# Down projection of the second token half by Strassen's seven products with a running sum each

## The chip, the cores and the metric

The kernel runs on one core of a Trainium2 chip. The metric is the device time of one execution in microseconds (us); lower is better.

## The reference

An adaLN block: attention with a layer norm and modulation from a condition vector, then a gated MLP with the same. Only the MLP's last step is touched.

```python
h = _layernorm(x, axis=-1) * (1 + cb) + sb            # x: 2048 tokens x 576
gate = jnp.einsum("bsd,df->bsf", h, W_gate)           # 576 x 4608
up = jnp.einsum("bsd,df->bsf", h, W_up)
gate = gate * (gate > 0)
x = x + gb * jnp.einsum("bsf,fd->bsd", gate * up, W_down)   # 4608 x 576
```

## The kernel before, in words

All matmuls run in a 4-byte format that keeps fewer bits than float32, so each operand is cut into `hi` (a cast, on ACT) and `lo` (the rest, a subtraction on POOL), and a product is three matmuls: hi by hi, hi by lo, lo by hi.

The MLP goes over the tokens in two halves of 1024, and in each half over the 4608 hidden columns in 18 blocks of 256: 36 blocks `m`, of which 18 to 35 (`m >= NFP`) are the second token half. A block has two column tiles `f` and two token quarters `k` of 512. Gate and up of a block are computed by Strassen's scheme (in Winograd's form) in seven products P1, P6, P2, P7, P5, P4, P3, in this order. Each product has a gate half (`xx` = 0) and an up half (`xx` = 1), written by `prod` into the two banks of one PSUM pair (tile `gu`); each half is 7 matmuls of 128x512. P2 adds onto P1's banks and P3 onto P5's.

`evac` empties a pair after both halves: P1 by an ACT copy into `q`, P6 and P7 by one DVE addition of 1024 columns, P2 by two DVE operations, P5, P4 and P3 by three of 512 columns each. P2, P5, P4 and P3 give the hidden tiles `r`, which `h_out` cuts into `hhi` and `hlo`.

The down projection of block `m` runs one block later, between the half-products of `m + 1`: 8 pieces `md_piece`, one for each 128 tokens, each of 12 matmuls 128x288 (two column halves, two `f`, three terms) into the pair `w` of pool `psW`, which has one buffer. DVE then adds the piece to `acc` (16 tiles of 128 x 576, residual and result). The down weights `wogb` are cut once in the first token half, stored in DRAM (`dk`) and loaded again in the second (`wd_prep`).

PE, DVE, ACT and POOL keep the order in which the code issues; semaphores come from the tiles that instructions share. `mat(m, s, fn)` places extra work in slot `s + 1` of block `m`, after the first half-product of that slot; `mlp_slots` writes the order out. SP issues the loads.

Of the kernel before, what the change touches and what calls it, by code (L numbers as in the profile page):

```python
# [21 lines left out]
NFT = F // P  # L22
# [3 lines left out]
H2 = D // 2  # L26
# [5 lines left out]
def kernel(  # L32
# [13 lines left out]
    nc = tc.nc  # L46
# [18 lines left out]
    dr = ctx.enter_context(tc.tile_pool(name="dr", bufs=1, space=bass.MemoryType.DRAM))  # L65
# [32 lines left out]
    acc = []  # L98
# [137 lines left out]
    mods = {}  # L236
# [185 lines left out]
    qhi, qlo, pthi, ptlo, ohi, olo = {}, {}, {}, {}, {}, {}  # L422
# [25 lines left out]
    st_, t4, t5, pt, hi_, lo_, bc, rb, rinv, ks_, pvps, done, o, bps = ({} for _ in range(14))  # L448
# [192 lines left out]
    NFP = NFT // 2  # L641
    NB = 2 * NFP
    ds_, hhi, hlo = {}, {}, {}
    wop, wraw, hop = {}, {}, {}
    pair, tmp = {}, {}

    def md_piece(m, k, qt, pool=None):
        b, fp = divmod(m, NFP)
        i = 8 * b + 4 * k + qt
        down_piece([hhi[m, f, k] for f in range(2)], [hlo[m, f, k] for f in range(2)],  # L650
                   [ds_[m, f] for f in range(2)], i, qt, f"md{m}_{k}_{qt}", pool=pool)()
        if fp == NFP - 1:
            nc.sync.dma_start(out[i * P:(i + 1) * P, :], acc[i])


    OPS = {"P1": ("A11", "B11"), "P2": ("A12", "B21"), "P6": ("S2", "T2"), "P7": ("S3", "T3"),
           "P5": ("S1", "T1"), "P4": ("A22", "T4"), "P3": ("S4", "B22")}
# [6 lines left out]
    dkeep = [dr.tile([P, 2, D], F32R, name=f"dk{f}") for f in range(NFT)]  # L664
    stores = []

    def flush_stores(left=0, eng=None):
# [258 lines left out]
    def prod(m, s, n, xx):  # L926

        hs, w = hop[m // NFP, OPS[s][1]], wop[n]
        ps = pair[m, s][:, xx, :]
# [10 lines left out]
    def h_out(m, f, k, r):  # L940
        pool, tag = HI[f, k]
        hi = hhi[m, f, k] = pool.tile([P, 512], F32R, tag=tag, name=f"hhi{m}_{f}{k}")
        if k == 0:
            pool, tag, w = op, "olo", 512
        elif f == 1:
            pool, tag, w = qp, ("qlo", "qhi")[m % 2], 512
        else:
            pool, tag, w = xp, "xm", 640
        lo = hlo[m, f, k] = pool.tile([P, w], F32R, tag=tag, name=f"hlo{m}_{f}{k}")[:, :512]
        nc.scalar.copy(hi, r)  # L950
        nc.gpsimd.tensor_sub(lo, r, hi.bitcast(F32))  # L951

    def gated(m, f, k, ps, r, a, op1=ALU.add):

        if a is None:
            nc.vector.tensor_scalar(r, ps[:, 0, :], 0.0, None, op0=ALU.max)
        else:
            nc.vector.tensor_tensor(r, ps[:, 0, :], a[:, 0, :], op=ALU.add)
            nc.vector.tensor_tensor(ps[:, 1, :], ps[:, 1, :], a[:, 1, :], op=op1)
        nc.vector.scalar_tensor_tensor(r, r, 0.0, ps[:, 1, :], op0=ALU.max, op1=ALU.mult)  # L960
        h_out(m, f, k, r)


    npair, px, free, kind = [0], {}, ["s", "s"], {}

# [5 lines left out]
    def new_pair(m, s):  # L971
        pair[m, s], kind[m, s] = new_banks(f"gu{npair[0]}")

    def evac(m, s):
        ps = pair[m, s]
        if s == "P1":
            t = tmp["q"] = pp.tile([P, 2, 512], F32, tag="hi", name=f"q{m}")
            nc.scalar.copy(t, ps)
        elif s == "P2":
            gated(m, 0, 0, ps, xp.tile([P, 640], F32, tag="xm", name=f"r{m}")[:, :512], None)  # L980
        elif s == "P6":
            nc.vector.tensor_tensor(tmp["q"], ps, tmp["q"], op=ALU.add)
        elif s == "P7":
            t = tmp["r"] = pp.tile([P, 2, 512], F32, tag="lo", name=f"r{m}", bufs=2)
            nc.vector.tensor_tensor(t, ps, tmp["q"], op=ALU.add)
            nc.scalar.copy(tmp["q"][:, 1, :], ps[:, 1, :])
        elif s == "P5":
            t = pp.tile([P, 2, 512], F32, tag="lo", name=f"c22_{m}", bufs=2)
            gated(m, 1, 1, ps, t[:, 0, :], tmp["r"])
        elif s == "P4":  # L990
            gated(m, 1, 0, ps, tmp["r"][:, 0, :], tmp["r"])
        else:

            gated(m, 0, 1, ps, tmp["q"][:, 0, :], tmp["q"], ALU.subtract)

    def wd_prep(m, f):
        tag = "wB" if f else "wC"
        k = 2 * (m % NFP) + f
        if m < NFP:
            load, gate, cut = prep_out(ds_, k, wd, "gb", (m, f), (None, tag))  # L1000

            def keep():
                cut()
                stores.append((dkeep[k], ds_[m, f][2]))

            return load, gate, keep

        def back():
            w = wp.tile([P, 2, D], F32R, tag=tag, name=f"wogb_{m}_{f}")
            ds_[m, f] = (w[:, 0, :], w[:, 1, :])  # L1010
            nc.sync.dma_start(w.bitcast(F32), dkeep[k].bitcast(F32))

        return [back]

# [171 lines left out]
    for i, ab in enumerate(lay0 + lay):  # L1186
        n = i - len(lay0) - 2 * NFT + 4
# [7 lines left out]
    for m in range(NB):  # L1195
        for f in range(2):
            for k, fn in enumerate(wd_prep(m, f)):
                if m >= NFP:
                    at_ = m, 3 * f
# [4 lines left out]
                mat(*at_, fn, sums=k == 1)  # L1204
    for i in range(4):
# [262 lines left out]
```

## Time and profile before

| what | value |
|---|---|
| runs | 2969.05, 2975.15, 2975.42 us; median 2975.15 us |
| span of the profiled execution | 2973.3 us (the page gives no other time for it) |
| PE busy over the span | 2895.3 us, 97% |
| DVE, ACT, POOL busy | 71%, 46%, 63% |
| second half's steady blocks (2500 to 2930 us) | PE 430.0 of 430 us, DVE 194.0, ACT 50.6, POOL 63.4 |

A timeline row has start, duration, engine, line, operation, output <- inputs and count; in brackets stand the idle time before it and the releaser. Matmuls are pipelined, so a row's duration reaches past the start of the next one; what PE needs is read from start to start.

### The profile page before, as it was taken

How to read it: one execution, taken by the hardware profiler on the slowest of the kernel's cores; microseconds unless marked ns; L12 is line 12 of the kernel's file. 1: busy time of each engine (PE TensorE's matmuls, PEld its weight loads, DVE VectorE, ACT ScalarE, POOL GpSimd, SP SyncE). 2: the span in 40 equal slices, each digit the busy share in tenths (PEclk: the TensorE clock that was granted, in tenths of full speed). 3: DMA queues.
4: the chain of work that ended last, by engine and by line, in shares of the span. 5: the costliest groups of instructions: out<-in, count | busy, mean ns of one | idle time of the engine just before them, and what ended most of it. 6: DMA issues, size and time to landing. Idle time of an engine off the chain costs nothing.

```text
span 2973.3 us, 41247 instructions
## 1 busy us (share of the span) xinstructions
PE 2895.3 (97%) x15448; PEld 2524.8 (85%) x15448; DVE 2108.3 (71%) x2894; ACT 1369.6 (46%) x1877; POOL 1866.1 (63%) x1309
## 2 busy tenths in 40 slices
PE   6889999999999999999999999999999999999999
PEld 5678888888888888888888788888878888888888
DVE  5778888788778888777889577777786444444444
ACT  3656666666676666666656333333323111111110
POOL 3767888888888889866777666678777211111111
PEclk8999999999999999999999999999999999999999
DMA  5312222222223223222243466668768844445443
GB/s 181 117 68 87 86 86 83 67 102 90 91 84 105 89 67 131 99 73 78 74 140 134 144 231 241 244 259 286 262 240 286 308 165 165 161 170 175 160 165 111
DMA packets 170759, 438.90 MB, mean 148 GB/s; under 512 B 15808, under 2 KB 62656, under 8 KB 170560
## 3 DMA queue, kind: packets, MB, share of 16 engines
q1 hardware_dynamic: 133200, 298.66, 30.3%
q10 hardware_dynamic: 37360, 137.61, 11.6%
q8 instruction: 122, 2.00, 0.3%
q14 instruction: 77, 0.63, 0.1%
HBM read 285.25 MB, written 179.27 MB: 156 GB/s over the span
## 4 chain that ended last, share of the span: by engine, by line
PE 86%; DVE 6%; POOL 3%; DMA 2%; ACT 2%; issue 2%; SPq 0%; ACTq 0%; DVEq 0%; POOLq 0%
PE gu L935 24%; PE md L590 15%; PE wo L590 13%; PE qps L387 12%; PE s L463 3%; PE s L462 3%; PE s L461 3%; PE pv L565 3%; PE pv L564 3%; PE pv L563 3%; DVE wr L741 2%; POOL lo L545 1%; PE qm L489 1%; DMA hop_T<-hk_T 1%; DVE t L466 1%
## 5 line engine op out<-in xcount | busy, mean ns | idle before, releaser
L545 POOL TENSOR_TENSOR lo<-p,hi 128x1024 fp32r<-128x1024 f32 x256 | 611.4, 2410 | 0.0
L554 POOL TENSOR_TENSOR ks<-ks,p 128x512 f32<-128x512 f32 x256 | 343.5, 1342 | 284.9 <-ACT p L538 211.4
L601 DVE TENSOR_TENSOR acc<-md,acc 128x576 f32<-128x576 f32 x288 | 217.7, 756 | 391.1 <-PE md L590 390.1
L590 PE MATMUL md<-wogb,hhi 128*128 128x288 f32 x2304 | 471.1, 297 | 14.3 <-DVE acc L601 14.3
L590 PEld LDWEIGHTS md<-wogb,hhi 128*128 128x128 f32 x2304 | 386.2, 189 | 39.6 <-DVE acc L601 18.5
L466 DVE TRANSPOSE_TENSOR_REDUCE t<-s 128x32 f32<-128x1024 f32 x256 | 316.2, 1243 | 136.0 <-PE s L463 125.0
L935 PE MATMUL gu<-hop_B,wop 128*128 128x512 f32 (+1 forms) x1512 | 373.1, 394 | 0.2
L590 PE MATMUL md<-wogb,hlo 128*128 128x288 f32 x1152 | 341.2, 296 | 0.0
L951 POOL TENSOR_TENSOR hlo<-r,hhi 128x512 fp32r<-128x512 f32 x72 | 93.7, 1301 | 372.4 <-issue 240.8
L935 PEld LDWEIGHTS gu<-hop_B,wop 128*128 128x128 f32 (+1 forms) x1512 | 279.8, 189 | 55.2 <-ACT lflh L920 0.9
L935 PE MATMUL gu<-hop_T,wop 128*128 128x512 f32 (+1 forms) x1260 | 314.3, 394 | 0.6 <-DMA wop<-wk_P 0.6
L536 DVE TENSOR_TENSOR p<-s,mb 128x1024 f32<-128x1024 f32 x250 | 295.3, 1219 | 4.2
L387 PE MATMUL qps<-hTa,wA 128*128 128x512 f32 x1176 | 285.7, 394 | 4.8 <-ACT wA L185 2.5
L590 PE MATMUL wo<-woga,ohi 128*128 128x288 f32 x1344 | 280.1, 302 | 0.0
L525 ACT CAST hi<-p 128x1024 fp32r<-128x1024 f32 x256 | 269.0, 1051 | 7.0
L538 ACT ACTIVATE p<-p 128x1024 f32<-128x1024 f32 x250 | 264.0, 1056 | 17.6 <-DVE p L536 15.7
L935 PEld LDWEIGHTS gu<-hop_T,wop 128*128 128x128 f32 (+1 forms) x1260 | 232.3, 189 | 44.2 <-DMA wop<-wk_P 1.0
L387 PEld LDWEIGHTS qps<-hTa,wA 128*128 128x128 f32 x1176 | 223.4, 190 | 53.4 <-ACT wA L185 2.9
L950 ACT CAST hhi<-r 128x512 fp32r<-128x512 f32 x72 | 44.7, 621 | 447.2 <-DVE r L960 443.8
L441 ACT ACTIVATE qhi<-qps 128x512 fp32r<-128x512 f32 x128 | 76.5, 597 | 341.8 <-PE qps L387 341.8
L590 PEld LDWEIGHTS wo<-woga,ohi 128*128 128x128 f32 x1344 | 218.8, 189 | 6.6
L590 PEld LDWEIGHTS md<-wogb,hlo 128*128 128x128 f32 x1152 | 217.4, 189 | 0.0
(207 smaller groups left out, 6408.4 us busy)
## 6 DMA issues: line engine op xcount, KB each, us to landing
wop<-wk_P SPq DMA_DIRECT2D x133, 640.0 KB
wk_P<-wop ACTq DMA_DIRECT2D x119, 640.0 KB
wr<-wlay SPq DMA_DIRECT2D x68, 384.0 KB
dk<-wogb ACTq DMA_DIRECT2D x36, 576.0 KB
wogb<-dk SPq DMA_DIRECT2D x36, 576.0 KB
againq<-akq SPq DMA_DIRECT2D x22, 640.0 KB
againo<-ako SPq DMA_DIRECT2D x18, 576.0 KB
rogb<-wd SPq DMA_DIRECT2D x36, 288.0 KB
```

The costliest lines, as they stand in the source:

```text
L387: return [lambda i=i, a=a, b=b: nc.tensor.matmul(ps, a, b, start=(i == 0), stop=(i == n - 1)) for i, (a, b) in enumerate(ops)]
L461: nc.tensor.matmul(ps, k[:, kt, :], qhi[u], start=True, stop=False)
L466: nc.vector.tensor_reduce(t4[u][:, 2 * h:2 * h + 2, :].rearrange("p k b -> p (k b)"), t.rearrange("p k (b j) -> p (k b) j", j=32), axis=AX ...
L525: nc.scalar.copy(hi_[u, h], pt[u, h])
L536: nc.vector.tensor_tensor(p, t, bc[u][:, None, :].to_broadcast([P, 2, 512]), op=ALU.subtract)
L538: nc.scalar.activation(p, p, AF.Exp, bias=0.0, scale=1.0)
L545: nc.gpsimd.tensor_sub(lo_[u, h], pt[u, h], hi_[u, h].bitcast(F32))
L554: nc.gpsimd.tensor_tensor(ks_[u], ks_[u], p[:, j, :], op=ALU.add)
L590: nc.tensor.matmul(ps[:, half, :H2], a[:, sl], w[b][:, cs], start=(n == 0 and seed is None), stop=(n == 5), skip_group_check=seed is not None)
L601: nc.vector.tensor_tensor(av, ps[:, :, :H2], av, op=ALU.add)
L935: nc.tensor.matmul(ps, a, c, start=s not in ("P2", "P3") and i == 0, stop=i == len(ops) - 1, skip_group_check=True)
L951: nc.gpsimd.tensor_sub(lo, r, hi.bitcast(F32))
```

## The change

For blocks 18 to 33 (`FAST`) the down projection is Strassen's too. The hidden block is 2 x 2 of (column tile, token quarter), the down weights 2 x 2 of (row tile, column half of 288). Seven products of 512 tokens by 288 columns take the place of eight: 84 matmuls 128x288 in a block instead of 96.

- **Pieces.** `fast_piece` makes 14 pieces of 6 matmuls, two column halves each: kind "4" (A22, two token groups), "16" (A11 and S2), "75" (S3 and S1), "23" (A12 and S4). One is issued after each half-product.
- **Running sums.** Each product is summed over the 16 blocks in a tile of its own: `acc` 0 to 7, free by then, take "16" and "75"; "4" and "23" go straight to `acc` 8 to 15. In the first such block ACT copies "16" and "75" into `acc`, later DVE adds. After block 33 `fast_end` mixes the sums on POOL and adds them on DVE, in slots of blocks 34 and 35.
- **Hidden tiles.** Four sums on POOL (S1, S2, S3, S4) and seven splits (`fast_split`) a block instead of four.
- **Weights.** The raw `wd` tile is loaded again, gated, combined and cut on POOL and ACT (`fast_weights`); `dk` keeps only the 4 tiles of blocks 34 and 35.
- **Evacuation.** In all blocks from 18, `evac_half` takes the place of `evac`: each half is emptied on its own, the first between the two half-products.

```diff
+    def fast_piece(m, kind, n):
+        if kind == "4":
+            specs = [(fop[m, "A22"], fw[m, "4"], 0, 2 * n + j) for j in range(2)]
+        else:
+            a, b = {"16": ("A11", "S2"), "75": ("S3", "S1"), "23": ("A12", "S4")}[kind]
+            specs = [(fop[m, x], fw[m, kind], j * H2, n) for j, x in enumerate((a, b))]
+        ps = psW.tile([P, 2, 512], F32, tag="w", name=f"mf{m}_{kind}_{n}")
+        for j, ((hi, lo), (whi, wlo), c, qt) in enumerate(specs):
+            sl = slice(qt * P, (qt + 1) * P)
+            for i, (x, w) in enumerate(((hi, whi), (hi, wlo), (lo, whi))):
+                nc.tensor.matmul(ps[:, j, :H2], x[:, sl], w[:, c:c + H2], start=i == 0, stop=i == 2)
...
+        if kind != "23" and m == FAST[0]:
+            nc.scalar.copy(a, ps[:, :, :H2])
+        else:
+            nc.vector.tensor_tensor(a, ps[:, :, :H2], a, op=ALU.add)
...
+    def fast_split(m, name, raw):
...
+        nc.scalar.copy(hi, raw)
+        nc.gpsimd.tensor_sub(lo, raw, hi.bitcast(F32))
...
+    def fast_weights(m):
...
+        mat(m - 1, 6, load)
+        mat(m, 0, lambda: gate(1))
+        mat(m, 1, lambda: gate(0))
+        mat(m, 1, sums1)
+        mat(m, 2, sums2)
+        mat(m, 2, cut4)
+        mat(m, 3, lambda: cut("16"))
+        mat(m + 1, 0, lambda: cut("75"))
+        mat(m + 1, 1, lambda: cut("23"))
+
+    def fast_end():
...
+        def put(n):
+            for a, b in ((acc[12 + n], acc[n]), (acc[8 + n], acc[4 + n])):
+                nc.vector.tensor_tensor(a, a, b, op=ALU.add)
...
+    def gated_half(x, ps, r, a, op1=ALU.add):
+        if x == 0:
+            if a is None:
+                nc.vector.tensor_scalar(r, ps[:, 0, :], 0.0, None, op0=ALU.max)
+            else:
+                nc.vector.tensor_tensor(r, ps[:, 0, :], a[:, 0, :], op=ALU.add)
+            return
+        if a is not None:
+            nc.vector.tensor_tensor(ps[:, 1, :], ps[:, 1, :], a[:, 1, :], op=op1)
+        nc.vector.scalar_tensor_tensor(r, r, 0.0, ps[:, 1, :], op0=ALU.max, op1=ALU.mult)
+
+    def fast_later(m):
...
+        nc.gpsimd.tensor_add(s1, r21, tmp[m, "r22"])
+        nc.gpsimd.tensor_sub(s2, s1, r11)
+        nc.gpsimd.tensor_sub(r11, r11, r21)
+        fast_split(m, "S2", s2)
+        fast_split(m, "S1", s1)
+        fast_split(m, "S3", r11)
...
+    def evac_half(m, s, x):
+        ps, fast = pair[m, s], m in FAST
+        if s == "P1":
+            if x == 0:
+                tmp[m, "q"] = pp.tile([P, 2, 512], F32, tag="hi", name=f"q{m}")
+            else:
+                nc.scalar.copy(tmp[m, "q"], ps)
+                if m - 1 in FAST:
+                    fast_last(m - 1)
+            return
+        q = tmp[m, "q"]
+        if s == "P6":
+            nc.vector.tensor_tensor(q[:, x, :], ps[:, x, :], q[:, x, :], op=ALU.add)
+            return
...
+            if m - 1 in FAST:
+                md = fast_pieces(m - 1)
...
                     others(m, i)
-                if m and i:
+                if m >= NFP:
+                    evac_half(m, s, 0)
+                if m and i or m - 1 in FAST:
                     md.pop(0)()
...
                 prod(m, s, 7 * m + i, 1)
                 wop.pop(7 * m + i)
-                if m and i < 2:
+                if m >= NFP:
+                    evac_half(m, s, 1)
+                if m and i < 2 or m - 1 in FAST:
                     md.pop(0)()
...
-                evac(m, s)
+                if m < NFP:
+                    evac(m, s)
```

How it moves instructions. First PE in a block of the second half, at product P5: the end of its first half, a down piece, the start of its second half. `gu` is the pair, `hop` the tokens' operand, `wop` the gate and up weights. In brackets stand the semaphores that an instruction waits for. Before:

```order
L935 MATMUL gu_24498<-hop_T_4_22907,wop_24434 128x512
L935 MATMUL gu_24498<-hop_T_2_22905,wop_24434 128x512
L590 MATMUL md_1_1_24510<-wogb_0_24121,hhi_01_24342 128x288 [waits DVE_49]
L590 MATMUL md_1_1_24510<-wogb_0_24121,hhi_01_24342 128x288
L590 MATMUL md_1_1_24510<-wogb_0_24121,hlo_01_24343 128x288
L590 MATMUL md_1_1_24510<-wogb_1_24240,hhi_11_24267 128x288 x2
L590 MATMUL md_1_1_24510<-wogb_1_24240,hlo_11_24268 128x288
L590 MATMUL md_1_1_24510<-wogb_0_24121,hhi_01_24342 128x288 x2
L590 MATMUL md_1_1_24510<-wogb_0_24121,hlo_01_24343 128x288
L590 MATMUL md_1_1_24510<-wogb_1_24240,hhi_11_24267 128x288 x2
L590 MATMUL md_1_1_24510<-wogb_1_24240,hlo_11_24268 128x288
L935 MATMUL gu_24498<-hop_T_0_22903,wop_24434 128x512 x2
```

Now, the same place (`mf_75` is a piece of kind "75", `fw` its weights, `fp_S` the split sums):

```order
L1043 MATMUL gu_24622<-hop_T_2_22840,wop_24539 128x512
L669 MATMUL mf_75_2_24637<-fw_75_24503,fp_S_24399 128x288 [waits DVE_49]
L669 MATMUL mf_75_2_24637<-fw_75_24503,fp_S_24399 128x288 x2
L669 MATMUL mf_75_2_24637<-fw_75_24503,fp_S_24396 128x288 x3
L1043 MATMUL gu_24622<-hop_T_0_22839,wop_24539 128x512 [waits DVE_49]
L1043 MATMUL gu_24622<-hop_T_0_22839,wop_24539 128x512
L1043 MATMUL gu_24622<-hop_T_3_22842,wop_24539 128x512
L1043 MATMUL gu_24622<-hop_T_1_22840,wop_24539 128x512 x2
```

The piece has six matmuls instead of twelve, and the second half's first matmul now waits for a DVE semaphore, the one that the evacuation of the first half of the same pair raises.

DVE in block 24, from a down piece's add before P2 to the evacuation of P5 (`r` and `c22` are hidden tiles). Before:

```order
L601 TENSOR_TENSOR acc11_136<-md23_0_3_24704,acc11_136 128x576
L956 TENSOR_SCALAR r24_24725<-gu128_24614 128x512
L960 SCALAR_TENSOR_TENSOR r24_24725<-r24_24725,gu128_24614 128x512
L601 TENSOR_TENSOR acc12_137<-md23_1_0_24742,acc12_137 128x576
L985 TENSOR_TENSOR r24_24763<-gu130_24732,q24_24645 128x1024
L601 TENSOR_TENSOR acc13_138<-md23_1_1_24778,acc13_138 128x576
L958 TENSOR_TENSOR c22_24_24799<-gu131_24766,r24_24763 128x512
L959 TENSOR_TENSOR gu131_24766<-gu131_24766,r24_24763 128x512
L960 SCALAR_TENSOR_TENSOR c22_24_24799<-c22_24_24799,gu131_24766 128x512
```

Now, the same stretch of block 25:

```order
L1074 TENSOR_SCALAR r25_25156<-gu133_25053 128x512
L679 TENSOR_TENSOR acc2_127<-mf24_16_2_25158,acc2_127 128x576
L1080 SCALAR_TENSOR_TENSOR r25_25156<-r25_25156,gu133_25053 128x512
L679 TENSOR_TENSOR acc3_128<-mf24_16_3_25178,acc3_128 128x576
L1115 TENSOR_TENSOR r25_25203<-gu135_25186,q25_25065 128x512
L679 TENSOR_TENSOR acc4_129<-mf24_75_0_25205,acc4_129 128x576
L1115 TENSOR_TENSOR r25_25203<-gu135_25186,q25_25065 128x512
L679 TENSOR_TENSOR acc5_130<-mf24_75_1_25222,acc5_130 128x576
L1076 TENSOR_TENSOR c22_25_25243<-gu136_25230,r25_25203 128x512
L679 TENSOR_TENSOR acc6_131<-mf24_75_2_25245,acc6_131 128x576
L1079 TENSOR_TENSOR gu136_25230<-gu136_25230,r25_25203 128x512
L1080 SCALAR_TENSOR_TENSOR c22_25_25243<-c22_25_25243,gu136_25230 128x512
```

An add now stands after each half's evacuation, and P7's one operation of 1024 columns has become two of 512.

ACT in block 19, where block 18's first pieces are emptied (`fh` are casts of hidden tiles, `fw` of weights):

```order
L1104 COPY q19_23241<-gu103_23229 128x1024
L695 CAST fh18_A12_23259<-q18_22946 128x512
L695 CAST fh18_S4_23264<-q18_22946 128x512
L734 CAST fw18_75_23287<-ft18_23030 128x576
L677 COPY acc0_125<-mf18_16_0_23292 128x576
L677 COPY acc1_126<-mf18_16_1_23308 128x576
L734 CAST fw18_23_23325<-fr18_22934 128x576
L677 COPY acc2_127<-mf18_16_2_23334 128x576
L695 CAST fh19_A22_23350<-r19_23332 128x512
L677 COPY acc3_128<-mf18_16_3_23354 128x576
```

The copies that free the pair `w` stand behind casts, of which S4's reads a sum that POOL makes; before, no such copy was on ACT.

More of the change, by code (lines that the diff above doesn't have):

```diff
@@ new lines, in fast_end, with mix @@
+    def fast_end():
+        def mix(n):
+            e1, e2 = acc[n], acc[4 + n]
+            nc.gpsimd.tensor_add(e1[:, H2:], e1[:, H2:], e1[:, :H2])
+            nc.gpsimd.tensor_add(e2[:, :H2], e2[:, :H2], e1[:, H2:])
+            nc.gpsimd.tensor_add(e1[:, H2:], e1[:, H2:], e2[:, H2:])
+            nc.gpsimd.tensor_add(e2[:, H2:], e2[:, H2:], e2[:, :H2])
+        def put(n):
+            for a, b in ((acc[12 + n], acc[n]), (acc[8 + n], acc[4 + n])):
+                nc.vector.tensor_tensor(a, a, b, op=ALU.add)
+        last = FAST[-1] + 1
+        for n in range(4):
+            mat(*((last, 5), (last, 6), (last + 1, 0), (last + 1, 1))[n], lambda n=n: mix(n))
+            mat(last + 1, 2 + n, lambda n=n: put(n))
@@ L663 @@
     wkeep = {(fp, s): dr.tile([P, 2, 5, P], F32R, name=f"wk{fp}_{s}") for fp in range(NFP) for s in OPS}
-    dkeep = [dr.tile([P, 2, D], F32R, name=f"dk{f}") for f in range(NFT)]
+    dkeep = [dr.tile([P, 2, D], F32R, name=f"dk{f}") for f in range(NFT - 2 * len(FAST))]
     stores = []
@@ new lines, in fast_later, with fast_last @@
+    def fast_later(m):
+        r21, s1 = tmp[m, "r"][:, 0, :], tmp[m, "r"][:, 1, :]
+        r11, s2 = tmp[m, "c"][:, 0, :], tmp[m, "c"][:, 1, :]
+        nc.gpsimd.tensor_add(s1, r21, tmp[m, "r22"])
[4 more added lines that the diff above has]
+        fast_split(m, "S3", r11)
+    def fast_last(m):
+        r12, s4 = tmp[m, "q"][:, 0, :], tmp[m, "q"][:, 1, :]
+        fast_split(m, "A12", r12)
+        nc.gpsimd.tensor_sub(s4, r12, tmp[m, "c"][:, 1, :])
+        fast_split(m, "S4", s4)
@@ new lines, in evac_half @@
+    def evac_half(m, s, x):
[3 more added lines that the diff above has]
+                tmp[m, "q"] = pp.tile([P, 2, 512], F32, tag="hi", name=f"q{m}")
+            else:
+                nc.scalar.copy(tmp[m, "q"], ps)
[5 more added lines that the diff above has]
+            nc.vector.tensor_tensor(q[:, x, :], ps[:, x, :], q[:, x, :], op=ALU.add)
+            return
+        if s == "P7":
+            if x == 0:
+                tmp[m, "r"] = pp.tile([P, 2, 512], F32, tag="lo", name=f"r{m}", bufs=2)
+            nc.vector.tensor_tensor(tmp[m, "r"][:, x, :], ps[:, x, :], q[:, x, :], op=ALU.add)
+            if x:
+                nc.scalar.copy(q[:, 1, :], ps[:, 1, :])
+            return
+        if s == "P2" and x == 0:
+            tmp[m, "r22"] = xp.tile([P, 640], F32, tag="xm", name=f"r{m}")[:, :512]
+        if s == "P5" and x == 0:
+            tmp[m, "c"] = pp.tile([P, 2, 512], F32, tag="lo", name=f"c22_{m}", bufs=2)
+        f, k, r, a, op1 = {"P2": lambda: (0, 0, tmp[m, "r22"], None, ALU.add),
+                           "P5": lambda: (1, 1, tmp[m, "c"][:, 0, :], tmp[m, "r"], ALU.add),
+                           "P4": lambda: (1, 0, tmp[m, "r"][:, 0, :], tmp[m, "r"], ALU.add),
+                           "P3": lambda: (0, 1, q[:, 0, :], q, ALU.subtract)}[s]()
+        gated_half(x, ps, r, a, op1)
+        if x == 0:
+            return
+        if not fast:
+            h_out(m, f, k, r)
+        elif s == "P2":
+            fast_split(m, "A22", r)
+        elif s == "P5":
+            fast_split(m, "A11", r)
+        elif s == "P4":
+            fast_later(m)
@@ L1003, in keep @@
                 cut()
-                stores.append((dkeep[k], ds_[m, f][2]))
+                if m + NFP not in FAST:
+                    stores.append((dkeep[k - 2 * len(FAST)], ds_[m, f][2]))
             return load, gate, keep
@@ L1195 @@
     for m in range(NB):
+        if m in FAST:
+            fast_weights(m)
+            continue
         for f in range(2):
```

53 lines of the change are left out of this document (51 added, 2 removed).

## The prediction

> **What bounds the kernel now.** I read the page's totals first, then the busy time by stage, then the chain of waits and the order of time in the stage that the change touches. In the stages, the columns are span, then busy time of PE, PEld, DVE, ACT, POOL, then PEclk, DMA share and GB/s.
>
> ```profile
> PE 2895.3 (97%) x15448; PEld 2524.8 (85%) x15448; DVE 2108.3 (71%) x2894; ACT 1369.6 (46%) x1877; POOL 1866.1 (63%) x1309
> 1750.00:2050.00 300.00, 296.28 (x1633) 260.15 (x1632) 212.05 (x240) 110.19 (x160) 207.32 (x191) 1.00 0.69 254
> 2160.00:2230.00 70.00, 63.09 (x333) 55.35 (x332) 57.85 (x47) 19.77 (x27) 54.72 (x47) 0.95 0.64 234
> 2500.00:2930.00 430.00, 430.00 (x2368) 381.11 (x2367) 193.96 (x255) 50.58 (x74) 63.38 (x49) 1.00 0.48 164
> ```
>
> The last row is the second token half of the MLP. PE has no gap in 430 us; DVE is at 45%, ACT at 12%, POOL at 15%. There each PE instruction removed is time saved, and each wait added to PE is time lost. The chain repeats the same piece once in each block m:
>
> ```profile
> 2531.78 4.83 PE gu L935 x21
> ...
> 2919.85 4.83 PE gu L935 x21
> ```
>
> Eleven blocks lie between, so a block is 388.07 / 11 = 35.28 us. What it is made of:
>
> ```profile
> 2642.28 0.43 PE L590 MATMUL md<-wogb,hhi 128*128 128x288 f32 x2
> 2642.48 1.01 ACT L978 COPY q<-gu 128x1024 f32<-128x1024 f32 x1 [0.28 <-PE gu L935]
> ...
> 2643.88 1.77 PE L935 MATMUL gu<-hop_T,wop 128*128 128x512 f32 x7
> 2644.08 0.76 DVE L601 TENSOR_TENSOR acc<-md,acc 128x576 f32<-128x576 f32 x1 [2.61 <-PE md L590]
> 2645.48 0.43 PE L590 MATMUL md<-wogb,hhi 128*128 128x288 f32 x2
> ```
>
> A down piece of 12 matmuls takes 2643.88 - 2642.28 = 1.60 us from start to start, a half-product of 7 takes 1.60 (1.605 in longer runs): 8 x 1.60 + 14 x 1.605 = 35.27, the block.
>
> **What is removed.** In 16 blocks 8 pieces of 12 matmuls become 14 of 6. By the rows above a piece of 6 is 0.80, and 14 x 0.80 = 11.2 instead of 12.8: 1.60 us a block, **25.6 us** in all. A block's two wogb loads become one raw load, and 32 dk stores go. No wait on these loads shows in the stage, so I count the DMA at nothing; 0.48 of DMA share is the cover, and it only falls.
>
> **What is added to POOL, ACT and DVE.** The prices:
>
> ```profile
> L951 POOL TENSOR_TENSOR hlo<-r,hhi 128x512 fp32r<-128x512 f32 x24 | 31.1, 1295 | 209.6 <-issue 167.4 <-ACT hhi L950 42.2
> L186 POOL TENSOR_TENSOR wogb<-rogb,wogb 128x576 fp32r<-128x576 f32 x17 | 24.1, 1420 | 0.0
> L950 ACT CAST hhi<-r 128x512 fp32r<-128x512 f32 x24 | 14.9, 621 | 209.9 <-DVE r L960 209.9
> L959 DVE TENSOR_TENSOR gu<-gu,r 128x512 f32<-128x512 f32 x17 | 11.9, 700 | 0.9
> L959 DVE TENSOR_TENSOR gu<-gu,r 128x512 f32<-128x512 f32 x24 | 16.8, 699 | 0.8
> ```
>
> POOL, a block: 7 splits and 4 sums of 512 (11 x 1.295), 2 gates and 3 cuts of 576 (5 x 1.42), 5 operations of 288 (estimated at half of 1.42 each): 14.2 + 7.1 + 3.6 = 24.9 us of 35. ACT: seven casts of 0.62 and the weights' casts, some 8 us. DVE: 12 adds of 0.76, four of 288 columns, 15 operations of about 0.69: 21 us. None is full. The last two rows are the same DVE operation beside a POOL at 69% (207.32 of 300) and at 15% (63.38 of 430): 700 and 699 ns, so more POOL work does not slow an operation that reads one bank and one SBUF tile, which all the steady ones are. POOL's queue has slack too. Its result that is wanted soonest after it is made is the cut of weights "75". P1's second half ends 9.9 us after P4's (four half-products, four pieces and P3's wait, below); then come the q copy and a cast on ACT (1.0 + 0.6), three POOL operations of 1.295 with a cast of 0.6 between, and the cut of 1.42: 17.5. The first piece that reads it stands three products on, at some 22.5. I count POOL and ACT at nothing in steady blocks; were those 5 us used up, PE would wait at that piece.
>
> **The new wait.** The order shows what the diff does not: the second half of each product waits for DVE's evacuation of the first half, though that lies in the other bank of the tile. Only a 6-matmul piece (0.80) stands between. The rows for the price of that round trip:
>
> ```profile
> 2663.11 3.38 PE L935 MATMUL gu<-hop_T,wop 128*128 128x512 f32 x14
> 2664.97 0.69 DVE L958 TENSOR_TENSOR c<-gu,r 128x512 f32<-128x512 f32 x1 [0.90 <-PE gu L935]
> ...
> 2669.52 1.78 PE L935 MATMUL gu<-hop_B,wop 128*128 128x512 f32 x7
> 2669.72 0.69 DVE L958 TENSOR_TENSOR r<-gu,r 128x512 f32<-128x512 f32 x1 [0.85 <-PE gu L935]
> 2670.45 0.70 DVE L959 TENSOR_TENSOR gu<-gu,r 128x512 f32<-128x512 f32 x1
> 2671.14 0.43 PE L590 MATMUL md<-wogb,hhi 128*128 128x288 f32 x2
> 2671.18 0.69 DVE L960 SCALAR_TENSOR_TENSOR r<-r,gu 128x512 f32<-128x512 f32 x1
> ```
>
> DVE starts 0.20 after PE goes on (2669.72 - 2669.52), or 0.26 where it waits for a second engine too (half of the fourteen ends at 2664.71; the operation starts at 2664.97). The operation takes 0.69 to 0.70. The way back:
>
> ```profile
> 2258.47 0.74 DVE L601 TENSOR_TENSOR acc<-md,acc 128x576 f32<-128x576 f32 x1
> 2259.26 0.54 PE L590 MATMUL md<-wogb,hhi 128*128 128x288 f32 x2 [0.62 <-DVE acc L601]
> ...
> 2260.97 1.78 PE L935 MATMUL gu<-hop_B,wop 128*128 128x512 f32 x7
> ```
>
> PE goes on 0.05 after DVE ends (2259.21 to 2259.26), and the piece then takes 1.71 instead of 1.60, since the weight load in front of a held matmul is no longer covered: 0.11 more. The same is seen at a product:
>
> ```profile
> 1916.37 1.28 POOL L713 TENSOR_TENSOR wop<-ws,wop 128x512 fp32r<-128x512 f32 x1
> 1917.41 0.79 PE L935 MATMUL gu<-hy_T,wop 128*128 128x512 f32 x2
> 1917.70 0.19 PEld L935 LDWEIGHTS gu<-hy_T,wop 128*128 128x128 f32 x1 [0.23 <-POOL wop L713]
> 1918.04 0.40 PE L935 MATMUL gu<-hz_T,wop 128*128 128x512 f32 x1
> ```
>
> POOL ends at 1917.65, the load starts at 1917.70, and the third matmul comes 0.63 after the first where 2 x 0.23 is usual.
>
> So a second half starts 0.20 + 0.70 + 0.16 = 1.06 after the first half's end, or 1.12; the piece covers 0.80. P2, P4 and P3 lose 0.26 each, P6, P7 and P5 (two engines waited for) 0.32 each, P1 nothing, since DVE does not evacuate its first half: 1.74 us a block. Behind DVE's evacuation on its queue stands the add of the piece; that comes 0.20 after the piece ends and finds DVE free.
>
> The bank pair psW has one buffer. After the second half of P5, P4 and P3 two DVE operations run first: 0.23 + 0.73 + 0.69, then the add of 0.76 ends 2.41 after the half's end and is seen 0.16 later, at 2.57; the next piece wants the bank after 0.80 + 1.605 = 2.405. That is 0.17 late. For P4 and P3 it vanishes inside the 1.06; P1 pays it. I take 0.15 a block, so **1.89 us** a block and 16 x 1.89 = **+30.2**. Blocks 18 and 35 still have 12-matmul pieces in those places (1.60, over 1.12) and lose nothing.
>
> **Once only.** In block 19 ACT instead of DVE empties the first eight pieces. Its copy price:
>
> ```profile
> L599 ACT COPY acc<-wo x232: 622/635/645, 121.5 to 1655.1; 128x576 f32<-128x576 f32 x116
> ```
>
> 0.635 is less than DVE's 0.76, but the copies are queued behind casts that wait for POOL. After P1 ends: q copy 1.01 and A12's cast 0.62, two POOL operations of 1.295, casts of S4 and "75" (1.3), then the copy: about 6 us, where the next piece wants the bank at about 5. Such a cast stands there again before "75". Between 0 and 10, I take **+4**: nearer the low end, since most of the eight copies have no POOL-bound cast ahead. At the end eight DVE additions of two SBUF tiles come ahead of evacuations in block 35; the nearest rows:
>
> ```profile
> L226 DVE TENSOR_TENSOR rogb<-rogb,mrow 128x576 f32<-128x576 f32 x17 | 26.3, 1545 | 0.0
> 2259.13 0.74 DVE L226 TENSOR_TENSOR rogb<-rogb,mrow 128x576 f32<-128x576 f32 x1
> ```
>
> Two of 0.74 fit except after P5 and P4, where DVE is some 0.85 late: **+2**; at 1.5 each it would be 8.
>
> Sum: -25.6 + 30.2 + 4 + 2 = **+10.6** on the span of 2973.3. The page gives no other time for its execution; the median of the runs is 1.85 above that span, so I forecast 2983.9 + 1.85, about **2985.7 us**.
>
> **The page's rule against this.** The Trainium skill (PSUM — Partial Sum Buffer, Summary: rules for kernel authors) asks for semaphores by bank, and calls a read from another bank than the one being written safe. By that rule the halves need not wait for one another, and the sum would be the first rival's; here the program, not the chip, makes them wait.
>
> **Rivals.** (1) *The evacuation is covered.* If PE did not in fact lose time at the second halves, the 25.6 would stay, less 2.4 for P1 and 6 once: -17, about 2958. It decides at the cover: the round trip would have to fall from 1.06 to 0.80. The rows above give 0.95 even without the uncovered weight load. Chance 0.08. (2) *Gain and waits cancel.* With 0.11 left out and 0.20 everywhere the loss is 6 x 0.15 = 0.9 a block, -11 in all; with about 0.25 for each product and little paid once, within 6 us of before. Chance 0.24. (3) *POOL becomes the bound.* 24.9 us would have to grow beyond 37, half again; then 3 us a block and +50, near 3035. Against it: 1295 ns here, and 1297 in the mean of the busy stage's hlo row:
>
> ```profile
> L951 POOL TENSOR_TENSOR hlo<-r,hhi 128x512 fp32r<-128x512 f32 x17 | 22.1, 1297 | 26.3 <-ACT hhi L950 17.1 <-DMA dk<-wogb 5.1 <-DMA rogb<-wd 3.3
> ```
>
> Chance 0.05. (4) *The clock drops.* Six short gaps a block; if the granted clock fell to the 0.95 of the stage at 2160, 16 blocks of 35.5 cost 30 us more, about 3015. That stage had one gap of over 5 us, the stage at 1750 only short ones and 1.00. Chance 0.04. The Trainium skill (TensorE: Matmul & The Clock Gate, A second HAM failure mode: psum-queue depth-cycling) describes such micro-idles between groups of matmuls letting the clock gate swing; the 1.00 beside short gaps speaks against it here.
>
> **How the numbers follow.** My forecast, slower by 6 to 28 us, has 0.58; rival 2 0.24, rival 1 0.08, rivals 3 and 4 0.09, 0.01 for a smaller gain. The bounds of the waits (0.9 and 2.3 a block) and of the single costs (0 and 18) give -11 to +29. 0.2% of this time is 6 us, about what a measurement can tell. The range 2970 to 3001 holds forecast and rival 2, 0.82. Faster 0.09, same 0.24, slower 0.67.
>
> **What would show it.** Right: in blocks 19 to 34 six gaps of PE before the second half, put down to DVE's evacuation, 0.2 to 0.35 us each; block about 35.6 us; DVE about 21 us a block; clock 1.00. Wrong: blocks near 33.8 us (the wait is covered), PE waiting for POOL (rival 3), or more than 10 us lost in block 19.

## The result and the profile after

The changed kernel takes 2994.98 us (median of 4 runs, 2994.54 to 2996.56), the kernel before 2972.1 us (median of 4, 2967.62 to 2975.42): a ratio of 1.0079, 95% interval 1.0065 to 1.0093. It is slower by 23 us, inside the range and 9 us above the forecast; the change is over twice the +10.6 us that were forecast. The profiled execution of the changed kernel has a span of 2992.5 us, against 2973.3.

The totals of the page after, then the windows of two stages of the kernel after (columns as in the prediction):

```profile
PE 2900.6 (97%) x15256; PEld 2496.2 (83%) x15256; DVE 2189.5 (73%) x3058; ACT 1431.7 (48%) x1997; POOL 2195.5 (73%) x1597
2350.00:2400.00 50.00, 43.95 (x217) 36.52 (x216) 18.05 (x28) 14.51 (x25) 28.21 (x24) 0.97 0.46 148
2500.00:2930.00 430.00, 428.10 (x2197) 356.33 (x2196) 251.56 (x375) 92.70 (x154) 291.00 (x244) 1.00 0.44 147
```

PE has 192 matmuls fewer (15448 before) and yet is busy 5 us longer in sum. In the steady stage POOL went from 15% to 68% and DVE from 45% to 59%; PE stays at 99.6%, its clock at 1.00. The place where PE stands idle is earlier, from 2350 to 2400: 6 us in 50.

A block starts where ACT copies its first product, P1, out of PSUM; blocks 18 and 20 start without a wait in ACT's own queue. A second mark is the start of block 18's last half-product on PE. The timelines of both engines, first of the kernel before (start of block 18, the mark, starts of blocks 20 and 35), then of the kernel after (start of block 18, the mark, starts of blocks 20 and 34):

```profile
2324.11 1.02 ACT L978 COPY q<-gu 128x1024 f32<-128x1024 f32 x1 [0.67 <-PE gu L935]
...
2355.21 4.99 PE L935 MATMUL gu<-hop_B,wop 128*128 128x512 f32 x21
...
2395.52 1.01 ACT L978 COPY q<-gu 128x1024 f32<-128x1024 f32 x1 [0.28 <-PE gu L935]
...
2924.72 1.01 ACT L978 COPY q<-gu 128x1024 f32<-128x1024 f32 x1 [0.28 <-PE gu L935]
```

```profile
2326.58 1.02 ACT L1104 COPY q<-gu 128x1024 f32<-128x1024 f32 x1 [0.73 <-PE gu L1043]
...
2359.12 3.38 PE L1043 MATMUL gu<-hop_B,wop 128*128 128x512 f32 x14
...
2408.73 1.01 ACT L1104 COPY q<-gu 128x1024 f32<-128x1024 f32 x1 [3.79 <-PE gu L1043]
...
2908.13 1.01 ACT L1104 COPY q<-gu 128x1024 f32<-128x1024 f32 x1 [3.82 <-PE gu L1043]
```

These rows divide the 19.2 us between the two spans. From block 19 on the start of a block lies 0.80 later in the kernel after, since a piece stands between P1's halves there; that is put back in block 34. Block 34 starts in the kernel before one block ahead of 2924.72, at 2889.44.

| Part of the span | Before | After | Difference | Forecast |
|---|---|---|---|---|
| to the start of block 18 | 2324.11 | 2326.58 | +2.5 | 0 |
| from there to block 18's last half-product | 31.10 | 32.54 | +1.4 | 0 |
| from there to the start of block 20 | 40.31 | 49.61 | +9.3 | +5.1 (0.8 mark, 0.3 steady, 4 once) |
| blocks 20 to 33, each | 35.28 | 35.67 | +0.39 (x14: +5.5) | +0.29 (x14: +4.1) |
| block 34 to the end | 83.86 | 84.37 | +0.5 | +1.5 (-0.8 mark, 0.3 steady, 2 once) |

The steady block after is (2908.13 - 2408.73) / 14 = 35.67. So the mechanism of the forecast is there at nearly its price, and the largest single cost was paid once, in block 19: 9.3 less 0.8 and 0.39 is 8.1 us.

**The steady block.** The timeline of PE after, at P7 and the first half of P5, then that of DVE at the same time (start, duration, engine and operation, the idle time before it):

```profile
2704.95 1.78 PE L1043 MATMUL gu<-hop_T,wop 128*128 128x512 f32 x7
2706.57 0.96 PE L669 MATMUL mf<-fw,fp_S 128*128 128x288 f32 x6
2707.58 1.88 PE L1043 MATMUL gu<-hop_T,wop 128*128 128x512 f32 x7
2709.30 0.96 PE L669 MATMUL mf<-fw,fp_S 128*128 128x288 f32 x6
2710.10 1.79 PE L1043 MATMUL gu<-hop_T,wop 128*128 128x512 f32 x7
```

```profile
2706.84 0.69 DVE L1115 TENSOR_TENSOR r<-gu,q 128x512 f32<-128x512 f32 x1 [0.93 <-PE gu L1043]
```

P7's first half takes 1.62 to the piece, the piece is done after 0.80 (as between 2709.30 and 2710.10), and the second half, which would start at 2707.37, starts at 2707.58: 0.05 after DVE's evacuation ends at 2707.53. It then takes 1.72 instead of 1.605. The loss at P7 is 0.21 + 0.11, the 0.32 of the forecast. The busy share of 99.6% does not show it, since a piece is counted with 0.96 though PE is through with it after 0.80; only the starts do.

### The profile page after: what moved, and what is told of

Same layout as the page of the kernel before. It is cut to its first block, busy times and chain, and to the rows that moved or that the text cites. A ratio compares the mean times of both kernels' runs of the same rounds, so it can differ in the third digit from the quotient of the medians.

```text
span 2992.5 us, 41535 instructions
## 1 busy us (share of the span) xinstructions
PE 2900.6 (97%) x15256; PEld 2496.2 (83%) x15256; DVE 2189.5 (73%) x3058; ACT 1431.7 (48%) x1997; POOL 2195.5 (73%) x1597
## 4 chain that ended last, share of the span: by engine, by line
PE 85%; DVE 7%; POOL 3%; issue 2%; ACT 2%; DMA 2%; ACTq 0%; SPq 0%; DVEq 0%; POOLq 0%
PE gu L1043 25%; PE wo L590 13%; PE qps L387 12%; PE md L590 8%; PE mf L669 5%; PE s L463 3%; PE s L462 3%; PE s L461 3%; PE pv L565 3%; PE pv L564 3%; PE pv L563 3%; DVE wr L849 2%; POOL lo L545 1%; PE qm L489 1%; DVE t L466 1%
## 5 line engine op out<-in xcount | busy, mean ns | idle before, releaser
L1043 PE MATMUL gu<-hop_B,wop 128*128 128x512 f32 (+1 forms) x1512 | 385.0, 398 | 0.4 <-DVE q L1076 0.2
L1043 PE MATMUL gu<-hop_T,wop 128*128 128x512 f32 (+1 forms) x1260 | 327.2, 399 | 5.3 <-DMA wop<-wk_P 1.9
L590 PE MATMUL md<-wogb,hhi 128*128 128x288 f32 x1280 | 263.9, 299 | 15.6 <-DVE acc L601 15.6
L538 ACT ACTIVATE p<-p 128x1024 f32<-128x1024 f32 x250 | 264.0, 1056 | 17.7 <-DVE p L536 15.8
L590 PEld LDWEIGHTS md<-wogb,hhi 128*128 128x128 f32 x1280 | 214.5, 190 | 31.1 <-DVE acc L601 20.2
L601 DVE TENSOR_TENSOR acc<-md,acc 128x576 f32<-128x576 f32 x160 | 120.8, 755 | 145.3 <-PE md L590 144.2
L590 PE MATMUL wo<-woga,olo 128*128 128x288 f32 x672 | 198.8, 296 | 0.4 <-POOL olo L579 0.2
L590 PE MATMUL md<-wogb,hlo 128*128 128x288 f32 x640 | 190.1, 297 | 0.0
L599 ACT COPY acc<-wo 128x576 f32<-128x576 f32 x232 | 147.6, 636 | 69.0 <-PE wo L590 65.1
L579 POOL TENSOR_TENSOR olo<-rb,ohi 128x512 fp32r<-128x512 f32 x128 | 167.2, 1307 | 17.1 <-ACT ohi L575 17.0
```

Source lines behind the costliest of these rows:

```text
L538: nc.scalar.activation(p, p, AF.Exp, bias=0.0, scale=1.0)
L579: nc.gpsimd.tensor_sub(olo[u], o.pop(u), ohi[u].bitcast(F32))
L590: nc.tensor.matmul(ps[:, half, :H2], a[:, sl], w[b][:, cs], start=(n == 0 and seed is None), stop=(n == 5), skip_group_check=seed is not None)
L599: nc.scalar.copy(av, ps[:, :, :H2])
L1043: nc.tensor.matmul(ps, a, c, start=s not in ("P2", "P3") and i == 0, stop=i == len(ops) - 1, skip_group_check=True)
```

## The experiments

The first four runs test two theories of the steady block: (A) PE waits at the second halves for DVE's evacuation of the first; (B) the halved evacuation itself, the smaller pieces or a busy POOL cost the time. The others look for the cause of what is lost once. Intervals are 95%, ratios against the kernel before.

### The evacuation of both halves after the second piece

```diff
-                if m >= NFP:
-                    evac_half(m, s, 0)
...
-                if m >= NFP:
-                    evac_half(m, s, 1)
...
                 if m < NFP:
                     evac(m, s)
+                else:
+                    evac_half(m, s, 0)
+                    evac_half(m, s, 1)
```

> The changed kernel with both halves of a product evacuated after its second piece, as before the change; nothing else moves. Theory W (the second half-products wait for the evacuation of the first halves, about 2 us a block): the waits on DVE in front of the second halves are gone, a steady block falls from 35.67 to about 33.7 us, and 16 blocks bring 31 us: span near 2961. Rival P (POOL, busy 291 of 430 us there, is late or in the way): POOL's work is the same, so a block stays at 35.5 to 35.7 and the span near 2992.

Measured: 2966.81 us, ratio 0.9986 (0.9976 to 0.9995), span 2962.8. The timeline of ACT in this kernel (blocks 21 and 34) and the window of its steady stage:

```profile
2441.05 1.02 ACT L1104 COPY q<-gu 128x1024 f32<-128x1024 f32 x1 [1.27 <-PE gu L1043]
...
2880.82 1.02 ACT L1104 COPY q<-gu 128x1024 f32<-128x1024 f32 x1 [1.27 <-PE gu L1043]
2500.00:2930.00 430.00, 430.00 (x2321) 376.26 (x2320) 254.27 (x392) 96.70 (x158) 307.24 (x263) 1.00 0.47 156
```

Thirteen blocks in 439.77 us: 33.83 each, and PE has no idle time in 430 us, with POOL at 71%. The early evacuation costs 35.67 - 33.83 = 1.84 us a block, P1's short wait for the bank included, and (A) holds. The engines do the same operations as in the changed kernel; only the evacuation's place in the program moved (DVE's, and at P1 and P7 also an ACT copy, with the operations on ACT and POOL that follow P1's). The span is 29.7 us shorter than the changed kernel's, of which 14 x 1.84 = 25.8 lie in the steady blocks. Blocks 18 and 19 still take 81.48 us (2325.74 to 2407.22, 82.15 in the changed kernel), so what is lost there has another cause.

### The same for three of the six products

```diff
-                if m >= NFP:
+                if m >= NFP and s not in ("P5", "P4", "P3"):
                     evac_half(m, s, 0)
```

and both halves after the second piece for these three.

> As the one before, but only P5, P4 and P3 are evacuated after the second piece; P6, P2 and P7 stay halved. Theory W: three of the six waits stay (P6 and P7 0.35, P2 0.29 with their restart), so a block is about 34.7 us and the span near 2977. P1's wait for the bank goes with the three. Rival P: no change, 2992.

Measured: 2978.37 us, ratio 1.0023 (1.0014 to 1.0033). ACT's timeline (thirteen blocks) and the waits of the weight loads, from 2420 to 2890, with us in total, times and the longest:

```profile
2445.95 1.02 ACT L1104 COPY q<-gu 128x1024 f32<-128x1024 f32 x1 [1.30 <-PE gu L1043]
...
2897.60 1.02 ACT L1104 COPY q<-gu 128x1024 f32<-128x1024 f32 x1 [1.29 <-PE gu L1043]
```

```profile
PEld gu L1043 <- DVE r L1115: 4.0, 14, 0.3
PEld gu L1043 <- DVE q L1110: 3.8, 13, 0.3
PEld gu L1043 <- DVE r L1074: 2.8, 13, 0.2
```

A block takes 34.74. No wait 33.83, three waits 34.74, six 35.67: 0.91 and 0.93 for three, or 0.31 us a wait. The three that are left are the first halves of P7, P6 and P2.

### The kernel before with halved evacuation

The kernel before, its pieces of twelve matmuls kept, and `gated_half` and `evac_half` called in the same places as in the change.

> The kernel before with the halved evacuation alone, no Strassen in the down projection. Theory W: the 12-matmul piece of 1.60 us covers the round trip of 1.06 to 1.12, so blocks stay at 35.28 and the span within 3 us of before. If instead the halving itself costs (more and shorter DVE instructions, one wait more on PE), blocks grow by 0.3 us or more and the span by 5 or more.

Measured: 2970.61 us, ratio 0.9998 (0.9989 to 1.0008).

```profile
2426.42 1.01 ACT L981 COPY q<-gu 128x1024 f32<-128x1024 f32 x1 [1.02 <-PE gu L935]
...
2885.06 1.01 ACT L981 COPY q<-gu 128x1024 f32<-128x1024 f32 x1 [1.02 <-PE gu L935]
```

Thirteen blocks at 35.28, the same as before. The span, 2968.9, is 4.4 us below the kernel before, more than the 3 expected; 3.9 of this lie ahead of block 18, where the two kernels are the same. The early evacuation costs nothing where 1.60 us of other work stands between the halves; with 0.80 it costs 1.84 a block. The cover decides, as the prediction put it.

### More work for POOL

```diff
+            for _ in range(4):
                 nc.gpsimd.tensor_sub(t[:, H2:D], w12, w11)
                 nc.gpsimd.tensor_sub(t[:, :H2], w22, w12)
```

> The changed kernel with the two first weight sums on POOL done four times over (six operations of 288 columns more, some 4.8 us of POOL a block; the result is the same). Theory W: POOL's queue has about 5 us of slack before PE wants its result, so a block stays at 35.67 or grows by at most 0.2, and the span by 0 to 4. Rival P: a block grows by a good part of the 4.8 us, the span by 30 or more.

Measured: 3002.58 us, ratio 1.0101 (1.0084 to 1.0118), span 3000.0: 7.5 us above the changed kernel's span, more than expected. The steady stage's window, the mark in block 18, ACT's copies at the start of blocks 20 and 34, and in block 19 an ACT cast and the PE wait behind it, with the clock after it:

```profile
2500.00:2930.00 430.00, 428.06 (x2195) 356.21 (x2194) 251.76 (x374) 92.40 (x156) 351.60 (x323) 1.00 0.45 147
2361.72 3.38 PE L1044 MATMUL gu<-hop_B,wop 128*128 128x512 f32 x14
...
2393.15 0.43 ACT L728 CAST fqhi<-fu 128x288 fp32r<-128x288 f32 x1 [6.08 <-POOL fu L723]
2394.17 1.06 PE L669 MATMUL mf<-fw,fp_S 128*128 128x288 f32 x6 [3.91 <-ACT acc L677]
2394.20:2398.00 3.80, 3.80 (x14) 3.14 (x15) 0.00 (x0) 1.62 (x3) 1.66 (x2) 0.63 0.02 4
...
2416.26 1.01 ACT L1105 COPY q<-gu 128x1024 f32<-128x1024 f32 x1 [3.79 <-PE gu L1044]
...
2915.54 1.01 ACT L1105 COPY q<-gu 128x1024 f32<-128x1024 f32 x1 [3.84 <-PE gu L1044]
```

With POOL at 82% the steady block, over fourteen blocks, is still 35.66: POOL has slack there. From the mark in block 18 to block 20 it takes 2416.26 - 2361.72 = 54.54 us instead of 49.61. The 4.9 more are lost at one place in block 19. There a cast on ACT waits 6.08 us for POOL (2.52 in the changed kernel), the copy that frees the piece's bank stands behind it, and PE waits 3.91 us (0.34). After that wait the granted clock falls, to 0.63 in the mean of 3.8 us, and the next half-product takes 2.87 us where the changed kernel's takes 1.62. Thus POOL is late in block 19 and nowhere after, and what is lost there grows with its work. (Block 18 also starts 3.4 us later, though the two kernels are the same up to there.)

### What holds POOL up in block 18

The timeline after shows why. First ACT's cast and POOL's subtraction that cut the weights "4" in block 18, then in block 19 the queue of ACT, and PE's wait for it:

```profile
2359.37 0.43 ACT L727 CAST fqhi<-fu 128x288 fp32r<-128x288 f32 x1 [18.54 <-PE md L590]
2359.88 0.80 POOL L728 TENSOR_TENSOR fqlo<-fu,fqhi 128x288 fp32r<-128x288 f32 x1 [16.04 <-ACT fqhi L727]
```

```profile
2373.82 0.62 ACT L695 CAST fh_S<-q 128x512 fp32r<-128x512 f32 x1 [4.11 <-POOL q L1095]
...
2374.92 0.63 ACT L677 COPY acc<-mf 128x576 f32<-128x576 f32 x1
2375.60 0.85 PE L669 MATMUL mf<-fw,fh_A 128*128 128x288 f32 x2 [3.75 <-ACT acc L677]
```

The tile of the new weights is the one in which block 17's hidden operand lies, and the last old down piece, which runs just ahead of the mark, still reads it. ACT waits 18.54 us for that piece, with P7's copy and the next casts queued behind; POOL, whose subtraction needs the cast, stands 16 us and is behind from there on. In block 19 a cast on ACT waits 4.11 us for POOL, the copy that empties a piece's bank stands behind it, and PE waits 3.75 us.

The wait costs more than itself. The timeline of PE behind it, and the window of the piece that waited, with the clock third from the end:

```profile
2377.21 2.56 PE L1043 MATMUL gu<-hop_B,wop 128*128 128x512 f32 x7
...
2379.60 0.43 PE L669 MATMUL mf<-fw,fh_A 128*128 128x288 f32 x2
2375.60:2377.20 1.60, 1.60 (x6) 1.60 (x7) 0.00 (x0) 0.00 (x0) 1.60 (x3) 0.50 0.00 0
```

The granted clock is 0.50 when PE goes on, and 1.00 again by 2379.1. The piece takes 2377.21 - 2375.60 = 1.61 us instead of 0.80, the half-product behind it 2.39 instead of 1.61: 1.6 us lost to the clock.

Two edits take the two links apart. One gives these weights a tile of their own in block 18:

```diff
-            hi, lo = (qp.tile([P, 512], F32R, tag=x, name=f"f{x}{m}")[:, :H2] for x in ("qhi", "qlo"))
+            if m == FAST[0]:
+                t4w = pp.tile([P, 2, 512], F32R, tag="hi", name=f"fq{m}")
+                hi, lo = t4w[:, 0, :H2], t4w[:, 1, :H2]
+            else:
+                hi, lo = (qp.tile([P, 512], F32R, tag=x, name=f"f{x}{m}")[:, :H2] for x in ("qhi", "qlo"))
```

> The changed kernel with block 18's weights of kind "4" in a tile of their own, so that ACT's cast does not wait for the last piece of block 17 (18.5 us in the changed kernel, with POOL idle for 16 us behind it). If that wait is what makes POOL late in block 19, blocks 18 and 19 together fall from 82.2 us to some 74 to 77, POOL's gap goes, and the long wait of a piece for ACT's copy (3.75 us) goes or falls below 1.5; span near 2986. If the copies on ACT alone cost the 10 us, they stay near 82.

The other leaves the wait and puts block 19's eight copies on DVE:

```diff
-            nc.scalar.copy(a, ps[:, :, :H2])
+            nc.vector.tensor_copy(a, ps[:, :, :H2])
```

> The changed kernel with the eight first copies of block 19 on DVE instead of ACT; block 18's tile as changed. If the queue of ACT (copies behind casts that wait for POOL) is what costs, the waits for ACT's copies (4.4 us) go and blocks 18 and 19 together fall from 82.2 to some 77; POOL's lateness stays, so a piece may then wait for POOL or for the casts instead, and some 2 to 4 us of the 10 remain. Span near 2987.

Measured, own tile: 2990.46 us, ratio 1.0071 (1.0058 to 1.0085). DVE copies: 2989.16 us, ratio 1.0066 (1.0049 to 1.0083). With the own tile, the start of block 18, a late load, the clock behind it, the cast of the weights "4", the mark and the start of block 20; with DVE copies, the start of block 18, the mark and the start of block 20:

```profile
2327.50 1.01 ACT L1108 COPY q<-gu 128x1024 f32<-128x1024 f32 x1 [0.40 <-PE gu L1047]
2342.68 2.92 PE L1047 MATMUL gu<-hop_T,wop 128*128 128x512 f32 x7 [1.92 <-DMA wop<-wk_P]
2344.00:2345.00 1.00, 1.00 (x4) 0.71 (x4) 0.00 (x0) 0.00 (x0) 0.92 (x2) 0.50 0.98 406
2345.17 0.43 ACT L731 CAST fq<-fu 128x288 fp32r<-128x288 f32 x1 [3.03 <-POOL fu L722]
2362.01 3.38 PE L1047 MATMUL gu<-hop_B,wop 128*128 128x512 f32 x14
2405.83 1.01 ACT L1108 COPY q<-gu 128x1024 f32<-128x1024 f32 x1 [3.82 <-PE gu L1047]
```

```profile
2326.54 1.01 ACT L1104 COPY q<-gu 128x1024 f32<-128x1024 f32 x1 [0.30 <-PE gu L1043]
...
2358.20 3.38 PE L1043 MATMUL gu<-hop_B,wop 128*128 128x512 f32 x14
...
2401.49 1.01 ACT L1104 COPY q<-gu 128x1024 f32<-128x1024 f32 x1 [3.82 <-PE gu L1043]
```

From the mark to block 20 it takes 43.82 us with the own tile and 43.29 with the DVE copies, where the changed kernel takes 49.61 and 41.5 would be free of loss (40.31 + 0.8 + 0.39). So the 8.1 us fall to 2.3 or to 1.8: either link broken takes away most of them. The cast comes 17.7 us after the start of block 18 with the own tile, 32.8 without. In both kernels the clock is 1.00 from 2350 to 2400, and no wait there is longer than 1.2 us. With the DVE copies the span is 2985.0, near the 2987 expected; with the own tile it is 2989.5 for the expected 2986. Counted from the start of block 18, the own tile missed what was expected (78.33 us to block 20): block 18 up to the mark takes 34.51 there, 32.54 in the changed kernel and 31.10 before. PE waits 1.9 us for the same load in the first two, but behind that wait the clock falls to 0.50 with the own tile (the window at 2344) and stays at 1.00 in the changed kernel; the half-product there and the piece after it take 4.88 us instead of 3.32. Why the clock falls in one and not in the other is not shown.

### All three, and the stores put back

The late evacuation, the own tile and the DVE copies together:

> Late evacuation, the tile of its own and the copies on DVE together. Steady blocks 33.83 as with late evacuation alone; blocks 18 and 19 together near 70.5 (36.1 and 33.8, and about 1 for a load) instead of 81.5. Span near 2952, some 20 us below the kernel before.

and the same with all `dk` stores of the kernel before in place again (the 32 that the change drops are never read):

```diff
-                if m + NFP not in FAST:
-                    stores.append((dkeep[k - 2 * len(FAST)], ds_[m, f][2]))
+                stores.append((dkeep[k], ds_[m, f][2]))
```

> The one before with the 32 stores of cut weights in the first token half put back (nothing reads them). Four runs without these stores reached block 18 at 2325.7 to 2330.0 us, two with them at 2320.2 and 2324.1. If the missing stores shift POOL and DVE against each other in block 10 (one DVE operation of 768 columns takes 5.7 us there without them, 1.5 to 1.8 with), block 18 begins at 2320 to 2324 here and the span is some 3 to 5 us below the one before, at 2948. If that was chance, the two are within 1.5 us.

Measured, all three: 2953.18 us, ratio 0.9947 (0.9935 to 0.9959), span 2951.3. With the stores: 2947.95 us, ratio 0.9933 (0.9918 to 0.9947), span 2945.8. The start of block 18, the mark and the start of block 20 with all three, then the start of block 18 with the stores:

```profile
2323.83 1.02 ACT L1108 COPY q<-gu 128x1024 f32<-128x1024 f32 x1 [0.50 <-PE gu L1047]
...
2356.06 3.38 PE L1047 MATMUL gu<-hop_B,wop 128*128 128x512 f32 x14
...
2395.71 1.02 ACT L1108 COPY q<-gu 128x1024 f32<-128x1024 f32 x1 [1.27 <-PE gu L1047]
```

```profile
2318.68 1.01 ACT L1108 COPY q<-gu 128x1024 f32<-128x1024 f32 x1 [1.77 <-PE gu L1047]
```

From the mark to block 20 it is 39.65 us, and 40.31 + 0.8 less the 1.45 that a block without waits gains is 39.66: nothing is lost in block 19. The span is the one expected; blocks 18 and 19 together take 71.88 us, 1.4 more than expected. With the stores the span is 2 us below the 2948 expected, and block 18 starts a little ahead of the 2320 to 2324. Both versions beat the kernel before and the changed one. Between the two the times overlap (one run with the stores took 2955.72), so the stores' part rests on where block 18 starts: 2324.11, 2320.17 and 2318.68 in the three kernels that keep them (before, before with halves, all three with stores), mean 2321.0; 2323.83 to 2330.00 in the seven that do not, mean 2327.0. That is some 6 us over the part of the span ahead of the new products. Each figure is one execution, though, and kernels that are the same up to block 18 differ there by 3.9 us (2324.11 and 2320.17) and by up to 6.2 (the seven). So the stores are the likely cause, and the size is not settled.

## Why the prediction was right, and where it was not

**The new wait: right.** Forecast 1.89 us a block, measured 1.84 by taking it away. By products, with 4.81 for two halves and two pieces without waits, the extra is 0.31 (P2), 0.34 (P7), 0.35 (P5), 0.27 (P4), 0.32 (P3) and 0.33 (P6), where 0.26 or 0.32 was forecast, and 0.08 at P1 for 0.15. (They add up to 2.00 and not 1.84, since without any wait a product takes 33.83 / 7 = 4.83.) The waits of the weight loads of the kernel after, over the whole stage, name the operations, among them (with 0.9 of block 19 in it):

```profile
PEld gu L1043 <- DVE q L1110: 5.3, 16, 0.9
```

**The gain: 0.15 a block too large.** Without waits a half-product and its piece take 33.83 / 14 = 2.416 us, not 2.405, so the smaller pieces bring 35.28 - 33.83 = 1.45 a block and not 1.60. That, and not the wait, is why the steady block came out at +0.39 instead of +0.29: 1.4 us in fourteen blocks. Why it takes these 0.01 us longer stays open.

**"+4" once in block 19: the mis-sized step.** It cost 8.1, within the 0 to 10 given. The step had the right queue, ACT's copies behind casts that wait for POOL, but priced POOL as on time. POOL was late, because the slack had been counted in steady blocks only and the tile of the first new weights had not been followed back to its last reader. From start to start on PE, against a steady block, 1.8 us go to the piece at P6, which waits for a hidden sum that POOL has not yet split, and to the half-product behind it; 3.9 to the wait for ACT's copy; 1.6 to the clock that fell after it; 1.0 to two shorter waits for ACT's copies. That is 8.3, of which 0.2 comes back elsewhere. The prediction had priced neither PE's own wait for POOL nor a fall of the clock here.

**"Blocks 18 and 35 ... lose nothing": right for the waits meant,** wrong by 1.4 us in block 18, where PE waits 1.9 us for a load of gate and up weights (0.58 before). "The DMA at nothing" missed that; the wait is there in all eight kernels with the change, 1.1 to 1.9 us at that load, against 0.58 and none in the two without. The share of 0.48 that was its cover holds in the steady blocks only: from 2326.6 to 2341.3, ahead of that wait, the DMA share is 1.05. It is 1.05 there before the change too (2324.1 to 2338), so what delays the load further was not settled.

**The stores "at nothing": probably wrong, by some 6 us in the mean.** They were taken as transfers that nobody waits for; what their absence changes in the first token half is told below. In the profiled executions of before and after, block 18 starts 2.5 us apart.

**The end: +2 forecast, about +0.9 measured** (0.5 + 0.8 for the mark, less the steady 0.39 of block 34).

**POOL and DVE at nothing in steady blocks: right.** 4.8 us more of POOL's work a block changed nothing, and the DVE add of the prediction still takes 700 ns beside a POOL at 68%. The group of lines after:

```profile
L1079 DVE TENSOR_TENSOR gu<-gu,r 128x512 f32<-128x512 f32 x25 | 17.5, 700 | 27.7 <-PE gu L1043 27.7
```

POOL's operation on 288 columns took 0.80 in block 18 (the row at 2359.88), not half of 1.42, with no effect.

**The rivals.** The wait is not covered (first rival); with the evacuation put later it is, and 2966.81 us came out, 9 above that rival's 2958 with the loss in block 19 still in it. Gain and waits nearly cancel in a block, to 0.39 us (second rival), but 14 or 16 times that and the single costs are more than 6 us. POOL bounds nothing (third), except once. The clock is 1.00 with six gaps of 0.2 us a block (fourth); among the new products it fell once, to 0.50, after the wait of 3.75 us in block 19, and that cost 1.6 us. The length of a wait alone did not decide it: after waits of 1.9 us for the load in block 18 it fell in two kernels (own tile, three products late) and not in the changed one. The swing that the Trainium skill describes (TensorE: Matmul & The Clock Gate, A second HAM failure mode: psum-queue depth-cycling) is not seen in 500 us of such gaps.

**What stays open.** That the program lets the second half wait for a read of the other bank of its tile is seen in every block. Whether two tiles of one bank each would free it was not tried. The Trainium skill (PSUM — Partial Sum Buffer, Summary: rules for kernel authors) has guards by bank; no run here has PE write one bank of a pair while DVE reads the other.

## What to carry to other kernels

When work between two dependent steps is halved, ask what it was hiding: a round trip of 1.06 us under 1.60 costs nothing, under 0.80 it costs 0.31 each time, and putting the evacuation after the second half brings it all back. Price the first and last passes of a new loop apart from the steady one, and for each tile that the new code reuses ask who read it last. A single wait can cost more than its length: here 3.75 us brought 1.6 more through the clock. A transfer that is never read may still matter to the engines beside it, so leave it out in a run of its own.

## What the hardware showed beyond that

One DVE operation at one place of the first token half, untouched by the change, takes about three times as long without the 32 stores. The timelines of DVE, of the kernel before and of the kernel after:

```profile
2050.89 1.76 DVE L741 TENSOR_TENSOR wr<-wr,wr 128x768 f32<-128x768 f32 x1
```

```profile
2050.36 5.69 DVE L849 TENSOR_TENSOR wr<-wr,wr 128x768 f32<-128x768 f32 x1
```

It is 5.69 to 5.73 us in all seven kernels without the stores and 1.49 to 2.16 in the three with them. One row of POOL's timeline beside it, of the kernel after:

```profile
2055.20 1.97 POOL L821 TENSOR_TENSOR wop<-wr,wop 128x512 fp32r<-128x512 f32 x1
```

Six operations of POOL, of which this is the last, follow one another from 2049.37 on almost without a gap, and the DVE operation, which reads two operands from SBUF, ends at 2056.05, inside this one, which takes 1.97 us where the same operation at 2049.37 takes 1.28. That each holds the other up is argued from these times, not shown; why the stores shift one against the other, and whether these 4 us are the same as the 6 ahead of block 18, stays open.
